# Transposing x in the DMA crossbar and splitting the w1 stream over two queues, in a squared-ReLU MLP kernel

## Chip, cores, metric

One core of one Trainium2 chip. The metric is device time in microseconds (us), median over runs. The profiler's span (first to last instruction) is about 2 us shorter than the time.

## The reference

```python
# x [1,2048,576]  w1 [576,4608]  b1 [4608]  w2 [4608,576]  b2 [576], all bf16
h = einsum("bsd,df->bsf", x, w1) + b1
h = relu(h) ** 2
out = einsum("bsf,fd->bsd", h, w2) + b2
```

x is cut into 4 blocks of 512 rows. For block n, phase An makes `hT` (the squared activations, features on partitions) and phase Bn multiplies by w2.

## The kernel before

576 is 9 chunks of 64, so phase A works with pairs of 64-row matmuls. `w1_h` holds the left 2304 columns of w1 on partitions 0 to 63 and the right 2304 on partitions 64 to 127. A step j makes 128 columns of each half:

```python
for c in range(NC):                       # NC = 9
    nc.tensor.matmul(bx[:], lhsT=w1_h[0:H, c, j*P:(j+1)*P], rhs=xT[0:H, c + 1, :], ...)
    nc.tensor.matmul(by[:], lhsT=w1_h[H:P, c, j*P:(j+1)*P], rhs=xT[H:P, c, :], ...)
```

Every 64-row chunk of x must thus lie transposed on both partition halves. The kernel before makes that with TensorE transposes of overlapping 128-column windows: 10 per row tile for blocks 0 and 1, and, for blocks 2 and 3, 5 per row tile plus two duplicating DMAs for every two row tiles, put into the middle of B0 and B1. All w1 loads go through one queue, in column order, lower half then upper half:

```python
def load_w1(j0, j1):
    for h in range(2):
        nc.sync.dma_start(out=w1_h[h*H:(h+1)*H, :, j0*P:j1*P],
                          in_=w1_v[:, :, h*FH + j0*P:h*FH + j1*P])
for (j0, j1) in [(0, 1), (1, 2), (2, 3), (3, 4), (4, 5), (5, 6)]:
    load_w1(j0, j1)
load_x_block(1, (nc.sync, nc.sync))
for (j0, j1) in [(6, 9), (9, 12), (12, 15), (15, 18)]:
    load_w1(j0, j1)
...
for j in range(NJ0):           a_step(0, j)     # NJ0 = 6
...                                             # 40 transposes of block 1
for j in range(NJ0, NJ1):      a_step(0, j)     # then A0 and A1 share each w1 column
for j in range(NJ0, NJ1):      a_step(1, j)
for j in range(NJ1, NJ):       a_step(0, j); a_step(1, j)
...
```

## Time and profile before

| | before |
|---|---|
| time, median (range) | 299.62 us (299.22 to 299.81) |
| span | 297.5 us |
| first phase-A matmul | 7.4 us |
| A0 with A1 | 73.2 us |
| B0, B1 | 36.5, 36.5 us |
| B2 with B3 | 70.7 us |

The page of the kernel before: busy time of each engine, TensorE's granted clock in tenths over 40 slices of the span, the DMA rate in the same slices, the queues, and the chain of work that ended last.

```profile
span 297.5 us, 5808 instructions
PE 292.7 (98%) x2574; PEld 184.8 (62%) x2574; DVE 79.0 (27%) x187; ACT 102.1 (34%) x161; POOL 8.9 (3%) x25
PEclk9999999999999999999999999999999999999999
GB/s 179 222 207 202 287 357 319 4 2 0 2 31 31 59 22 15 7 0 3 0 2 57 44 20 22 20 2 0 2 0 2 20 22 21 2 20 22 20 22 21
...
q1 hardware_dynamic: 21056, 15.19, 20.7%
q0 software_dynamic: 480, 1.19, 2.0%
...
PE 98%; DVE 0%; ACT 0%; issue 0%
```

TensorE (PE) is the bound: it has 98% of the chain, and no other engine reaches 1%. Only work taken from PE, without a new wait for it, can pay. The list of PE's waits says the same; its columns are total us, number of waits, longest:

```profile
PE wps L81 <- DVE wz L77: 1.3, 1, 1.3
PE ph L175 <- DVE xTw L128: 0.2, 1, 0.2
```

PE's transposes are what can be taken away. From the chain in order of time (start us, us, what), B0 with two of its transpose bursts:

```profile
80.57 4.52 PE po L198 x36
85.08 0.56 PE tp L148 x10
85.64 8.82 PE po L198 x72
94.46 0.56 PE tp L148 x10
95.02 22.05 PE po L198 x180
```

### The profile page before, as it was taken

The numbers are of one execution on the slowest core, as the hardware profiler recorded it, in microseconds if no ns is written. First come the engines' busy times: TensorE is split into PE (matmuls) and PEld (weight loads), VectorE is DVE, ScalarE is ACT, GpSimd is POOL, SyncE is SP. The second block draws the span as 40 slices with busy tenths as digits, with TensorE's granted clock in tenths as the row PEclk, the third lists the DMA queues.
The fourth block names the chain that finished last, engine by engine and source line by source line (L and its number), as shares of the span: only waits on it lengthen the run. The fifth ranks groups of instructions, "written<-read, shape, count | busy, mean of one in ns | idle before, by whom it ended". The sixth has DMA issues, their size and how long they took to land.

```text
span 297.5 us, 5808 instructions
## 1 busy us (share of the span) xinstructions
PE 292.7 (98%) x2574; PEld 184.8 (62%) x2574; DVE 79.0 (27%) x187; ACT 102.1 (34%) x161; POOL 8.9 (3%) x25
## 2 busy tenths in 40 slices
PE   7999999999999999999999999999999999999995
PEld 5564444444488876444468887544447778777774
DVE  3353444444401111444431001244441111101111
ACT  4575666666611000666641100266661000000000
POOL 3000000000010100000001100000000000000000
PEclk9999999999999999999999999999999999999999
DMA  8999999000011200000002200000000000000000
GB/s 179 222 207 202 287 357 319 4 2 0 2 31 31 59 22 15 7 0 3 0 2 57 44 20 22 20 2 0 2 0 2 20 22 21 2 20 22 20 22 21
DMA packets 21849, 17.04 MB, mean 57 GB/s; under 512 B 7924, under 2 KB 21504, under 8 KB 21824
## 3 DMA queue, kind: packets, MB, share of 16 engines
q1 hardware_dynamic: 21056, 15.19, 20.7%
q0 software_dynamic: 480, 1.19, 2.0%
q8 instruction: 20, 0.33, 0.5%
q10 hardware_dynamic: 288, 0.30, 0.3%
q14 instruction: 5, 0.04, 0.0%
HBM read 13.13 MB, written 2.36 MB: 52 GB/s over the span
## 4 chain that ended last, share of the span: by engine, by line
PE 98%; DVE 0%; ACT 0%; issue 0%
PE po L198 48%; PE ph L175 27%; PE ph L177 20%; PE tp L138 1%; PE wps L81 1%; PE tp L148 1%; ACT r L181 0%; ACT xTw L126 0%; DVE xTw L128 0%; DVE o_sb L207 0%; DVE wz L77 0%
## 5 line engine op out<-in xcount | busy, mean ns | idle before, releaser
L198 PE MATMUL po<-w_sb,hT 128*128 128x288 bf16 x1152 | 142.3, 286 | 0.0
L175 PE MATMUL ph<-xTw,w_h 64*128 64x512 bf16 x648 | 140.7, 376 | 0.2 <-DVE xTw L128 0.2
L177 PE MATMUL ph<-xTw,w_h 64*128 64x512 bf16 x648 | 140.5, 376 | 0.0
L198 PEld LDWEIGHTS <-hT 128*128 128x128 bf16 x1152 | 112.3, 98 | 29.3 <-issue 1.3
L181 ACT ACTIVATE r<-ph,b1T 128x512 bf16<-128x512 f32 x144 | 91.2, 684 | 95.0 <-PE ph L177 74.2
L175 PEld LDWEIGHTS <-w_h 64*128 64x128 bf16 x648 | 60.7, 94 | 43.9 <-issue 0.5
L182 DVE TENSOR_TENSOR hT<-r 128x512 bf16<-128x512 bf16 x144 | 61.2, 425 | 83.2 <-ACT r L181 83.1
L177 PEld LDWEIGHTS <-w_h 64*128 64x128 bf16 x648 | 60.6, 94 | 32.1 <-issue 0.2
L207 DVE TENSOR_TENSOR o_sb<-po,b_bc 128x288 bf16<-128x288 f32 x32 | 13.2, 452 | 127.3 <-PE po L198 127.3
L126 ACT COPY xTw<-tp 128x640 bf16<-128x640 bf16 x15 | 9.6, 695 | 26.0 <-PE tp L148 23.5
L154 POOL DMA_DIRECT2D xTw<-xTw x4 | 2.5, 627 | 141.2 <-ACT xTw L126 141.2
L138 PEld LDWEIGHTS <-x_sb 128*128 128x128 bf16 x80 | 5.7, 112 | 1.6 <-POOL warm L108 0.9
L138 PE MATMUL tp<-ident,x_sb 128*128 128x128 bf16 x80 | 6.1, 244 | 0.1
L128 DVE COPY xTw<-tp 128x640 bf16<-128x640 bf16 x9 | 4.3, 490 | 4.5 <-PE tp L138 4.2
L81 PE MATMUL wps<-wz 128*128 128x512 bf16 x5 | 2.3, 629 | 1.3 <-DVE wz L77 1.3
L148 PE MATMUL tp<-ident,x_sb 128*128 128x128 bf16 x40 | 2.9, 219 | 0.0
L155 POOL DMA_DIRECT2D xTw<-xTw x4 | 2.7, 676 | 0.0
L148 PEld LDWEIGHTS <-x_sb 128*128 128x128 bf16 x40 | 2.6, 98 | 0.2
L81 PEld LDWEIGHTS <-wz 128*128 128x128 bf16 x5 | 0.6, 134 | 2.1 <-DVE wz L77 1.3
L109 ACT ACT_TABLE_LOAD x1 | 1.3, 1283 | 1.7 <-PEq L284 1.7
L63 POOL MEMSET x_sb<- 128x256 bf16 x4 | 1.3, 319 | 18.8 <-PE tp L138 14.6
L64 POOL MEMSET x_sb<- 128x256 bf16 x4 | 1.3, 318 | 0.0
(14 smaller groups left out, 2.9 us busy)
## 6 DMA issues: line engine op xcount, KB each, us to landing
w_sb<-in_w_dram SPq DMA_DIRECT2D x6, 864.0 KB, 11.4
w_h<-in_w_dram SPq DMA_DIRECT2D x8, 432.0 KB, 11.7
out_dram<-o_sb SPq DMA_DIRECT2D x15, 144.0 KB, 1.8
w_h<-in_w_dram SPq DMA_DIRECT2D x12, 144.0 KB, 4.2
x_sb<-in_x_dram SPq DMA_DIRECT2D x6, 288.0 KB, 8.0
xTw<-xTw POOLq DMA_DIRECT2D x4, 160.0 KB, 2.6
xTw<-xTw POOLq DMA_DIRECT2D x4, 128.0 KB, 2.4
x_sb<-in_x_dram SPq DMA_DIRECT2D x2, 144.0 KB, 2.9
```

The costliest lines, as they stand in the source:

```text
L81: nc.tensor.matmul(wps[:], lhsT=wz[:, 0:P], rhs=wz[:, P:640], start=(i == 0), stop=(i == NWARM - 1))
L126: last_act_copy[0] = nc.scalar.copy(out=dst, in_=src)
L128: nc.vector.tensor_copy(out=dst, in_=src)
L138: nc.tensor.transpose(tp[:, i, :], xs[:, j, w * H:w * H + P], ident[:])
L148: nc.tensor.transpose(tp[:, n, :], xs[:, j, w * H:w * H + P], ident[:])
L155: eng.dma_start(out=xv[H:P, 0:NH, 0, cols], in_=xv[0:H, 0:NH, 1, cols])
L175: nc.tensor.matmul(bx[:], lhsT=w1_h[0:H, c, j * P:(j + 1) * P], rhs=xT[0:H, c + 1, :], start=(c == 0), stop=(c == NC - 1))
L177: nc.tensor.matmul(by[:], lhsT=w1_h[H:P, c, j * P:(j + 1) * P], rhs=xT[H:P, c, :], start=(c == 0), stop=(c == NC - 1))
L181: nc.scalar.activation(out=r[:], in_=bank[:], func=ACT.Relu, bias=b1T[:, ft:ft + 1], scale=1.0)
L182: nc.vector.tensor_tensor(out=hT[:, ft, :], in0=r[:], in1=r[:], op=ALU.mult)
L198: nc.tensor.matmul(po[h][:, 0:DH], lhsT=hT[:, ft, jj * P:(jj + 1) * P], rhs=w2_sb[:, ft, h * DH:(h + 1) * DH], start=(i == 0), stop=(i == ...
L207: nc.vector.tensor_tensor(out=o_sb[:, h * DH:(h + 1) * DH], in0=po[h][:, 0:DH], in1=b2_bc[:, h * DH:(h + 1) * DH], op=ALU.add,)
```

## The change

Intent: take 88 of the 120 x transposes off TensorE. Blocks 1 to 3 are transposed by the DMA crossbar on their way from DRAM, and small copies fill the ninth window. Block 0 keeps TensorE, with 8 transposes a row tile. Phases run A0 A1 B0 A2 B1 A3 B2 B3, A0 and A1 no longer mixed. The w1 halves go to two queues, so as to load faster: lower on SP (`nc.sync`), upper on POOL (`nc.gpsimd`) after two chunks on ACT. In the diff, comments and the text in brackets stand for code that is left out.

```diff
-    for (j0, j1) in [(0, 1), (1, 2), (2, 3), (3, 4), (4, 5), (5, 6)]:
-        load_w1(j0, j1)
-    load_x_block(1, (nc.sync, nc.sync))
-    for (j0, j1) in [(6, 9), (9, 12), (12, 15), (15, 18)]:
-        load_w1(j0, j1)
+    CH = [(0, 1), (1, 2), (2, 4), (4, 6), (6, 10), (10, 14), (14, 18)]
+    for (j0, j1) in CH[:2]:
+        load_w1(nc.sync, 0, j0, j1)
+        load_w1(nc.scalar, 1, j0, j1)
+    for (j0, j1) in CH[2:]:
+        load_w1(nc.sync, 0, j0, j1)
+        load_w1(nc.gpsimd, 1, j0, j1)
 ...
+    def load_xT(sb):
+        alloc_xT(sb)
+        xT = xT_blk[sb]
+        rows = x2[sb * SB:(sb + 1) * SB, :]
+        nc.sync.dma_start_transpose(out=xT[:, 0:NK, :], in_=rows[:, 0:2 * H * NK])
+        nc.sync.dma_start_transpose(out=xT[:, NK:2 * NK, :], in_=rows[:, H:H + 2 * H * NK])
+        nc.sync.dma_start(out=xT[0:H, 2 * NK, :], in_=xT[H:P, 2 * NK - 1, :])
+        nc.sync.dma_start(out=xT[H:P, 2 * NK, :], in_=xT[0:H, 0, :])
 ...
+    # block 0, per row tile: 4 + 4 transposes, and copies of (128 x 512) and (64 x 128)
 ...
-    (A0 and A1 interleaved; make_mid: transposes of blocks 2, 3 inside B0, B1)
+    load_xT(1); (b2, w2 loads on SP); load_xT(2)
+    phase_a(0); phase_a(1)
+    phase_b(0, hTs[0]); load_xT(3)
+    phase_a(2); phase_b(1, hTs[1]); phase_a(3); phase_b(2, hTs[2])
     phase_b(3, hTs[3], last=True)
```

## The prediction

> **What bounds the kernel now.** TensorE. The page shows PE 98% busy (292.7 of 297.5 us) and the chain of waits 98% on PE, clock 1.0 throughout. Stages, from the chain in order of time: head to the first phase-A matmul 7.4 us; A0 with A1 73.1; B0 36.5; A2 35.1; B1 36.5; A3 35.1; B2+B3 70.7; tail 3. A matmul pair of phase A starts every 0.216 us, so 18 steps of 9 pairs are 34.95 us: A2 and A3 run at that pace. B2+B3 gives 35.35 us for a B phase without transposes.
>
> **What the change removes.** On PE: the 40 transposes of block 1 (A0+A1 take 73.1 us against 2 x 35.05: 3.0 us), the 40 of blocks 2 and 3 inside B0 and B1 (36.5 against 35.35 twice: 2.3 us; the chain shows four bursts of 0.56 us), and 8 of 40 in the head. All but the last sit on the critical path, because PE never idles there: **5.3 us**. Off the path go 10 ACT copies of 693 ns, 4 DVE copies, 8 memsets and POOL's 8 duplicating DMAs. Matmuls, B-phase additions and output stores stay.
>
> **What it adds.** *Head:* the ninth window is now made by separate small copies. DVE copies of 128x640 took 490 ns; I estimate 0.42 us for 128x512 and 0.2 for 64x128, five of each: 3.1 us against 2.5. ACT likewise three pairs, estimated 0.85 us each against 0.69. DVE becomes the pacer from 4.35 us on and uses up what 8 fewer transposes give; ACT's windows are read only from the fifth pair on. Head: 0 to +0.2 us.
>
> *w1:* A0 now runs alone, so it consumes 288 KB a step of 1.94 us, 148 GB/s, until 42 us, where before A1 steps halved the need. The table of windows shows 216 GB/s from 7.4 to 19.1 us. Each load wrote 64 partitions. The Trainium skill, "SBUF — State Buffer" (Door 1: The DMA port swizzle), says that 64 partitions reach 8 of 16 ports, about 218 GB/s; the 216 agrees. The halves on two queues can use both sets. The tightest chunk is columns 6 to 10: 3.5 MB with x block 0; at 216 GB/s landed near 20 us, needed near 19; at 280 GB/s landed near 16. I expect no stall or under 1 us.
>
> *Crossbar:* 1.05 MB per block. "DMA: Bandwidth & Descriptors" (Latency and other measured facts) gives 261 GB/s, hence an estimate of 4 us a block, plus two dependent copies of about 2.5 us (POOL's landed in that). Block 1 is wanted at 42 us, block 2 at 114, block 3 at 186: tens of us of slack. SP waits for the transposes before issuing w2, which is needed from 77 us and took 14 us of issue. Off the path.
>
> **Sum.** 299.76 - 5.3 + 0.1 (head) + 0.0 to 0.8 (stall, mean 0.1): **294.6 us**, 1.7% faster; range **293.4 to 296.8**. Chances: faster by over 2% 0.12, within 2% 0.83, slower 0.05.
>
> **What would show each step.** Right: PE transposes fall from 120 (plus b1) to 32; A0+A1 last about 70.1 us, B0 and B1 35.35 each, A2 and A3 unchanged; the first phase-A matmul starts at 7.3 to 7.7 us; crossbar transposes land long before their readers; DMA well over 216 GB/s in 7 to 20 us; PE never idle in the body. Wrong: PE waits on w1 inside A0, or on transposed x at 42 us.
>
> **What would make it wrong.** (a) POOL-issued w1 loads lagging behind SP's, stalling A0 near chunks 2-4 or 6-10: +1 to +4 us. (b) Crossbar transposes many times slower than estimated, or slowing the w1 stream. (c) A stall long enough to lower the granted clock. (d) PE starting earlier than I think, by up to 0.6 us, which without a stall comes close to the 2% line (293.8).

## The result, and the profile after

| | before | after |
|---|---|---|
| time, median (range) | 299.62 us (299.22 to 299.81) | 305.22 us (303.38 to 305.25) |
| span, mean granted clock | 297.5 us, 1.000 | 303.4 us, 0.989 |
| first phase-A matmul | 7.4 us | 8.6 us |
| A0 with A1 | 73.2 us | 79.6 us |
| B0, B1 | 36.5, 36.5 us | 35.4, 35.4 us |

The ratio is 1.017, interval 1.014 to 1.020. The kernel got slower: the change is clear of noise and of the other sign than predicted, but under 2%; the time lies outside the predicted range.

The same parts of the page, after:

```profile
span 303.4 us, 5600 instructions
PE 289.3 (95%) x2486; PEld 178.2 (59%) x2486; DVE 78.3 (26%) x188; ACT 95.1 (31%) x152; POOL 5.3 (2%) x14
PEclk9968999999999999999999999999999999999999
GB/s 185 229 213 172 175 338 352 146 158 9 2 0 2 19 22 19 22 0 3 2 0 2 19 22 19 19 2 2 0 2 0 22 19 23 0 22 19 22 19 19
...
q1 hardware_dynamic: 24688, 14.31, 20.2%
q0 software_dynamic: 704, 2.37, 3.4%
q10 hardware_dynamic: 1472, 0.59, 0.9%
...
PE 92%; DMA 6%; DVE 0%; issue 0%
PE po L176 47%; PE ph L156 45%; DMA w_h<-in_w_dram 5%; DMA x_sb<-in_x_dram 1%; PE ph L158 1%; DVE o_sb L185 0%
```

The clock falls in slices 3 and 4, and w1 loads have come onto the chain. The waits of PE, after:

```profile
PE ph L156 <- DMA w_h<-in_w_dram: 9.2, 3, 5.7
PE wps L73 <- DVE wz L69: 1.3, 1, 1.3
```

All of it lies in A0's first columns. PE's timeline, where only lines that begin after idle time are copied (last bracket: us idle before, and who ended it):

```profile
8.59 0.39 PE L156 MATMUL ph<-xTw,w_h 64*128 64x512 bf16 x1 [2.74 <-DMA w_h<-in_w_dram]
...
11.38 0.39 PE L156 MATMUL ph<-xTw,w_h 64*128 64x512 bf16 x1 [0.68 <-DMA w_h<-in_w_dram]
...
19.24 0.61 PE L156 MATMUL ph<-xTw,w_h 64*128 64x512 bf16 x1 [5.74 <-DMA w_h<-in_w_dram]
```

The wait at 19.24 us is the one for chunk 2-4. After it a matmul takes 0.61 us: the clock is at half. B0 and everything after A0 run as predicted; in the chain, B0 is now one unbroken piece:

```profile
88.16 35.39 PE po L176 x288
123.54 0.32 PE ph L156
```

When did each w1 chunk land? These times come from the semaphore that each load raises (issue, then landing, in us; needed is when PE would read it at full pace from 7.3 us on):

```
columns   lower half (SP)     upper half             needed
0-1        1.66 ->  8.54      ACT   1.67 ->  7.72      7.3
1-2        2.44 -> 11.33      ACT   2.38 -> 10.06      9.2
2-4        3.61 -> 19.19      POOL  2.20 ->  7.99     11.2
4-6        4.25 -> 21.89      POOL  2.95 -> 11.05     15.1
6-10       4.95 -> 24.95      POOL  3.68 -> 14.82     18.9
10-14      7.62 -> 28.85      POOL  4.40 -> 17.74     26.7
14-18     14.77 -> 30.77      POOL  5.13 -> 20.67     34.5
```

POOL's upper halves come early, and SP's lower halves come late. I had named "POOL-issued w1 loads lagging behind SP's" as a risk. It is the reverse. Counting the trace's DMA packets by queue shows why; between 12 and 18 us:

```
SP    333 packets, mean  492 B,  27 GB/s
POOL  329 packets, mean 3686 B, 202 GB/s
```

The two queues get the same number of packets and very unequal bytes. The Trainium skill, "DMA: Bandwidth & Descriptors" (Queues, rings and completion order), says that a DMA engine goes round its queues packet by packet. The near-equal counts agree. The page's queue lines show the sizes: q0 (POOL's queue) moved 2.37 MB in 704 packets, about 3.4 KB each; q10 (ACT's) 0.59 MB in 1472, about 0.4 KB. A packet of SP or ACT holds one contiguous run, and one of POOL gathers several, up to 4 KB here.

**Theory T1**: turns are taken by packet, so POOL's big packets starve SP's small ones; PE waits for SP's half, and the long wait halves the clock. **Rivals**: R1, A0 without A1 needs w1 faster than any one queue brings it (the order is at fault); R2, the crossbar transposes on SP slow the w1 stream; T1b, any second queue starves SP, whatever its packets; T1c, SP starves because the other queue is filled early with later columns.

### The profile page after: what moved, and what is told of

Its sections match the earlier page's. It is cut to its first block, busy times and chain, and to the rows that moved or that the text cites. A ratio compares the mean times of both kernels' runs of the same rounds, so it can differ in the third digit from the quotient of the medians.

```text
span 303.4 us, 5600 instructions
## 1 busy us (share of the span) xinstructions
PE 289.3 (95%) x2486; PEld 178.2 (59%) x2486; DVE 78.3 (26%) x188; ACT 95.1 (31%) x152; POOL 5.3 (2%) x14
## 3 DMA queue, kind: packets, MB, share of 16 engines
q0 software_dynamic: 704, 2.37, 3.4%
q10 hardware_dynamic: 1472, 0.59, 0.9%
## 4 chain that ended last, share of the span: by engine, by line
PE 92%; DMA 6%; DVE 0%; issue 0%
PE po L176 47%; PE ph L156 45%; DMA w_h<-in_w_dram 5%; DMA x_sb<-in_x_dram 1%; PE ph L158 1%; DVE o_sb L185 0%
## 5 line engine op out<-in xcount | busy, mean ns | idle before, releaser
L156 PE MATMUL ph<-xTw,w_h 64*128 64x512 bf16 x648 | 143.4, 381 | 9.2 <-DMA w_h<-in_w_dram 9.2
L158 PE MATMUL ph<-xTw,w_h 64*128 64x512 bf16 x648 | 143.4, 382 | 0.0
L156 PEld LDWEIGHTS <-w_h 64*128 64x128 bf16 x648 | 61.2, 95 | 88.7 <-DMA w_h<-in_w_dram 10.3
L158 PEld LDWEIGHTS <-w_h 64*128 64x128 bf16 x648 | 61.4, 95 | 0.0
L65 POOL DMA_DIRECT2D w_h<-in_w_dram x5 | 3.7, 780 | 0.0
L123 DVE COPY xTw<-ta 128x512 bf16<-128x512 bf16 x4 | 1.7, 425 | 3.0 <-PE ta L122 2.9
L132 ACT COPY xTw<-tb 128x512 bf16<-128x512 bf16 x3 | 1.8, 585 | 0.4 <-PE tb L127 0.4
L122 PE MATMUL ta<-ident,x_sb 128*128 128x128 bf16 x16 | 1.8, 242 | 0.0
L127 PE MATMUL tb<-ident,x_sb 128*128 128x128 bf16 x16 | 1.7, 239 | 0.0
L122 PEld LDWEIGHTS <-x_sb 128*128 128x128 bf16 x16 | 1.2, 109 | 0.8 <-DMA x_sb<-in_x_dram 0.8
L127 PEld LDWEIGHTS <-x_sb 128*128 128x128 bf16 x16 | 1.3, 111 | 0.0
L124 DVE COPY xTw<-ta 64x128 bf16<-64x128 bf16 x4 | 0.9, 218 | 0.1
L133 ACT COPY xTw<-tb 64x128 bf16<-64x128 bf16 x3 | 0.8, 262 | 0.0
```

The costliest lines, as they stand in the source:

```text
L65: eng.dma_start(out=w1_h[h * H:(h + 1) * H, :, j0 * P:j1 * P], in_=w1_v[:, :, h * FH + j0 * P:h * FH + j1 * P])
L122: nc.tensor.transpose(ta[:, k, :], xs[:, j, 2 * H * k:2 * H * k + P], ident[:])
L123: nc.vector.tensor_copy(out=xT0[:, 0:NK, cols], in_=ta[:, :, :])
L127: nc.tensor.transpose(tb[:, k, :], xs[:, j, H + 2 * H * k:H + 2 * H * k + P], ident[:])
L132: nc.scalar.copy(out=xT0[:, NK:2 * NK, cols], in_=tb[:, :, :])
L156: nc.tensor.matmul(bx[:], lhsT=w1_h[0:H, cl, j * P:(j + 1) * P], rhs=xT[0:H, wl, :], start=(i == 0), stop=(i == NC - 1))
```

## The experiments

All eight gave outputs that agree with the reference. Kernels of one set shared a chip and the runs of the kernel before.

### e1_all_sp: all w1 on SP

```diff
-        load_w1(nc.scalar, 1, j0, j1)
+        load_w1(nc.sync, 1, j0, j1)
 ...
-        load_w1(nc.gpsimd, 1, j0, j1)
+        load_w1(nc.sync, 1, j0, j1)
```

> The changed kernel with all w1 halves on SP, in column order, same chunks. Theory T1 (the POOL queue's packets of about 3.7 KB take turns one for one with SP's packets of about 0.5 KB, so SP's lower halves starve): the waits at columns 2-4 vanish; first phase-A matmul at 7.3 to 7.7 us; at 195 to 200 GB/s chunk 6-10 lands near 20 us against a need at 19, so at most about 1.5 us of stall; no half clock; 294.3 to 296.0 us. Rival R1 (A0 alone needs w1 faster than any single queue brings it, so the A0-first order is at fault): stalls of 4 us or more remain, 299 us or more. Rival R2 (the crossbar transposes on SP slow w1): unchanged stalls, since the transposes stay on SP.

Measured: 295.52 us (294.59 to 296.30), before 299.91; ratio 0.986 (0.983 to 0.988). Clock 1.0. The first phase-A matmul starts at 7.23 us and the waits at columns 0 to 2 are gone. PE's waits:

```profile
PE ph L158 <- DMA w_h<-in_w_dram: 1.6, 1, 1.6
PE wps L73 <- DVE wz L69: 1.3, 1, 1.3
PE ph L156 <- DVE xTw L123: 0.6, 1, 0.6
```

The wait of 1.6 us is for chunk 6-10, whose upper half landed at 20.83 us. Order and crossbar are as in the change, so R1 and R2 fall as the main cause: at most this 1.6 us can be R1's.

### e2_swap: lower half on ACT and POOL, upper on SP

```diff
 (two lines joined into one)
-        load_w1(nc.sync, 0, j0, j1);  load_w1(nc.gpsimd, 1, j0, j1)
+        load_w1(nc.sync, 1, j0, j1);  load_w1(nc.gpsimd, 0, j0, j1)
 (the first two chunks likewise, with nc.scalar)
```

> The changed kernel with the halves swapped: lower on ACT and POOL, upper on SP. T1: the same stall, now for the upper half; 303 to 306.5 us, POOL's chunks land by about 21 us in order while SP's chunk 2-4 lands near 19 us. A rival that blames the lower half's partitions or its place in DRAM expects a clearly different time (under 300).

Measured: 306.19 us (304.89 to 307.35), ratio 1.023. SP's chunk 2-4, now the upper half, landed at 19.23 us; POOL's landed in order by 21.20. PE now waits mostly at L158, the upper matmul (5.9 us), where in the change it waited at L156. From 12 to 18 us SP had 333 packets and POOL 330. The queue decides, not the half.

### e3_before_pool: the kernel before, upper halves on POOL

```diff
-            nc.sync.dma_start(out=w1_h[h * H:(h + 1) * H, ...
+            eng = nc.gpsimd if h == 1 and j0 >= 2 else nc.sync
+            eng.dma_start(out=w1_h[h * H:(h + 1) * H, ...
```

> The kernel before with one thing changed: upper w1 halves from column 2 on go to POOL's queue. T1: SP's lower halves starve in it too: PE waits for w1 at column 2, half clock after it if the wait is over about 3 us, 303 to 311 us. R1 (order at fault) and R2 (crossbar at fault): nothing of either is in this kernel, so 299 to 301 us.

Measured: 310.65 us (308.52 to 311.04), ratio 1.035. This one edit costs the kernel before 10.7 us: PE waits 7.8 us for w1 where it waited for none, and the clock halves in the longest wait, of 3.98 us:

```profile
PE ph L176 <- DMA w_h<-in_w_dram: 5.8, 2, 4.0
PE ph L178 <- DMA w_h<-in_w_dram: 2.0, 2, 1.8
```

From 14 to 19 us SP sends runs of 256 B, and it had 268 packets and 13.6 GB/s against POOL's 249 and 200. The stall needs neither the new order nor the crossbar.

### e4_act: chunks 2-4 and 4-6 of the upper half on ACT, the later ones on SP

```diff
-        load_w1(nc.gpsimd, 1, j0, j1)
+        load_w1(nc.scalar if j0 < 6 else nc.sync, 1, j0, j1)
```

> The changed kernel with upper chunks 2-4 and 4-6 on ACT's queue (packets of the same size as SP's) and the later ones on SP. T1: both halves of 2-4 land within 1.5 us of each other at about 10 to 12 us, no half clock, 294.3 to 297 us. A rival T1b (any second queue starves SP, whatever the packet size): SP's 2-4 lands after 15 us, over 300 us. For the step of the prediction that two queues reach more ports: over 230 GB/s between 5 and 12 us if true, about 200 if not.

Measured: 295.53 us (294.95 to 295.67), ratio 0.986. Chunk 2-4 landed at 10.23 (SP) and 11.06 us (ACT), 4-6 at 12.73 and 14.00. T1b falls: a second queue with packets of SP's size takes its share and no more. PE never waited for w1; it waited 0.9 us once for an ACT copy, which ACT's longer issuing had delayed. The total was 230 GB/s from 4 to 6 us, 195 from 6 to 8 and 215 from 8 to 12, hardly above one queue's 203, so the gain in rate that I had expected from two queues did not show here.

### e5_fine: all w1 on SP, in finer chunks

```diff
 (on e1_all_sp)
-    CH = [(0, 1), (1, 2), (2, 4), (4, 6), (6, 10), (10, 14), (14, 18)]
+    CH = [(0, 1), (1, 2), (2, 3), (3, 4), (4, 5), (5, 6),
+          (6, 8), (8, 10), (10, 12), (12, 14), (14, 16), (16, 18)]
```

> All w1 on SP as in e1_all_sp, with one column a load up to column 6 and two after that. T1: e1's only stall (1.6 us before column 6) came from the four-column chunk that must land whole; at 200 GB/s columns 6-8 now land near 17 us against a need at 18.9, so PE never waits for w1; 293.4 to 294.7 us, which is what the prediction's sum gave without its stall term (294.5). If A0-first order were at fault beyond chunk size, a stall of 1 us or more stays, over 295.

Measured: **293.78 us** (293.72 to 293.92), before 299.93; ratio 0.980 (0.978 to 0.982). It is faster than the kernel before, clear of noise; whether by 2% is unclear, since the interval holds 0.98. Lines of the page, the list of PE's waits, and lines of the chain: the start of A0, then those that begin where A1, B0 and A2 end:

```profile
span 292.0 us, 5608 instructions
PEclk9999999999999999999999999999999999999999
PE 97%; DVE 1%; issue 0%
```

```profile
PE wps L73 <- DVE wz L69: 1.3, 1, 1.3
PE ph L156 <- DVE xTw L123: 0.6, 1, 0.6
```

```profile
7.28 0.37 PE ph L156
...
77.39 35.39 PE po L176 x288
112.78 0.32 PE ph L156
...
147.85 35.39 PE po L176 x288
```

No wait for w1 is left (chunk 6-8 landed by 18.03 us, needed at 18.9), so R1 falls altogether: A0 alone is served by one queue at about 200 GB/s, if the chunks are small enough to land in time.

### e6_keep_clock: dummy matmuls in the stall

```diff
 (on the change, in phase_a)
+            if sb == 0 and j == 2:
+                fill = ps_o.tile([P, 512], FP32, name="fill", tag="po")
+                for i in range(26):
+                    nc.tensor.matmul(fill[:], lhsT=wz[:, 0:P], rhs=wz[:, P:640], ...)
             a_step(sb, j)
```

> The changed kernel with 26 dummy matmuls (26 x 0.216 = 5.6 us of work on zeros) put between columns 1 and 2 of A0, in the time that TensorE idled. If the half clock after the stall is caused by the idle time and costs what I worked out (12.5 pairs of 0.427 against 0.216 us, 2.65 us): clock 1.0 throughout, 302.0 to 303.4 us. If the idle time is not its cause: 305 or more.

Measured: 302.88 us (302.57 to 304.06), ratio 1.011; mean clock 0.998. In another set the change itself took 305.22 (its ratio 1.017). B0 started at 86.11 us against 88.16, although SP's chunk 2-4 landed 0.66 us later in this run (19.85 against 19.19). So the idle time causes the half clock, and keeping PE busy returns 2 to 3 us of the loss. It does not return the wait. The Trainium skill, "TensorE: Matmul & The Clock Gate" (Part 1), says that an idle window of about 3.4 us puts the clock to half. The runs agree in the main: idle times of 5.74 us (the change) and 3.98 us (e3) were followed by half clock, those of 2.74 and 1.8 us were not. The figure is not a sharp limit: the clock fell 4.4 us into the idle time of the change, and 2.7 us into that of e3 (at 22.26 us, PE idle since 19.54). In the change the clock is 0.99 in the first of these stretches, in whose last 4.5 us PE idles, and 0.50 in the second:

```profile
12.00:18.00 6.00, 1.50 (x14) 0.49 (x10) 1.28 (x3) 1.26 (x2) 0.00 (x0) 0.99 1.06 229
18.00:20.00 2.00, 0.76 (x4) 0.28 (x6) 0.00 (x0) 0.00 (x0) 0.00 (x0) 0.50 1.12 217
```

(Columns of this table of windows: stretch, its length, busy us with instruction counts of PE, PEld, DVE, ACT and POOL, granted clock, DMA share, GB/s.)

### m1_meter: the queues by themselves

```diff
 (on e1_all_sp, added at the end; the results of these loads are not read; some lines joined)
+    halves(nc.sync, [], nc.sync, QS);  all_parts()      # QS: four chunks of 1 KB runs
+    halves(nc.sync, QS, nc.scalar, QS);  all_parts()    # halves: 64 partitions each
+    halves(nc.sync, QS, nc.gpsimd, QS);  all_parts()    # all_parts: 1 KB runs, 128 partitions
+    halves(nc.sync, [(2, 18)], nc.gpsimd, QS)           # SP: 4 KB runs
```

> Not a candidate: e1_all_sp, and after the last output w1 is loaded again in groups, to meter the queues (the time is over 60 us longer; outputs stay right). (1) upper half alone on SP, 1 KB runs: 190 to 200 GB/s. (2) the same runs over 128 partitions, SP alone: about 350 GB/s if the number of partitions limits group 1, about 200 if the 1 KB runs of DRAM do. (3) lower on SP beside upper on ACT: 300 GB/s or more if the halves on two queues use both port sets as the prediction had it; about 200 to 220 if not. (4) lower on SP in 1 KB runs beside upper on POOL: if turns are taken by packet, equal packet counts, POOL 3.5 to 4 KB a packet and SP 1 KB, so SP gets about a fifth. (5) lower on SP in 4 KB runs beside POOL: SP's share rises to 45 to 55% by the same rule; if POOL has priority for another reason, SP stays near a fifth.

The groups did not run one after the other: each load waited only for its own columns, and the first began at 199 us, so its time (323.40 us) means nothing and its groups overlapped. I read stretches, picked after the run, in which the packet records show the named queues alone. GB/s by queue:

```
SP alone, 64 partitions, 1 KB runs (222-223 us)        193
SP alone, 128 partitions, 1 KB runs (220-221 us)       381
SP beside ACT, 1 KB runs each (235-237 us)             184 + 186
SP 1 KB beside POOL (276-278): 99 and 92 packets        50 + 188
SP 4 KB beside POOL (310-312): 83 and 85 packets       170 + 174
```

In the fourth row 34 of SP's 99 packets are output stores, of 1152 B; the rest are loads. Single microseconds scatter: SP alone with 64 partitions also shows 253 GB/s (202-203 us). Over longer stretches the rates are steady: 202 from 14 to 20 us of e1_all_sp (64 partitions), 357 from 46 to 50 us of e5_fine (w2, 128 partitions).

The totals of four of these stretches in the table of windows:

```profile
220.00:221.00 1.00, 1.00 (x13) 0.47 (x10) 0.00 (x0) 0.00 (x0) 0.00 (x0) 1.00 1.08 381
235.00:237.00 2.00, 2.00 (x13) 0.79 (x10) 0.43 (x1) 0.08 (x1) 0.40 (x1) 0.50 1.07 370
276.00:278.00 2.00, 2.00 (x19) 1.58 (x17) 0.00 (x0) 0.00 (x0) 0.00 (x0) 1.00 1.03 239
310.00:312.00 2.00, 2.00 (x19) 1.58 (x17) 0.00 (x0) 0.00 (x0) 0.00 (x0) 1.00 1.02 344
```

The last two lines are the direct test of T1. With 1 KB packets SP got 21% of the bytes beside POOL; with 4 KB packets it got 49%. The packet counts were near equal both times. POOL has no priority; it has larger packets. The first line shows, against 193 GB/s, that 64 partitions had half the rate of 128; the second, that two queues of equal packets can have both halves' rates at once.

### e8_act_all: every upper half on ACT

```diff
-        load_w1(nc.gpsimd, 1, j0, j1)
+        load_w1(nc.scalar, 1, j0, j1)
 ...
-        if j == 0:      # which engine makes block 0's second copies
+        if True:        # always DVE: ACT is busy issuing
```

> The changed kernel with every upper w1 half on ACT's queue in place of POOL's, all queued early as POOL's were, and the head's ACT copies moved to DVE (ACT is busy issuing until about 12 us). Packets of both queues are then of one size. T1: SP's lower halves keep step with ACT's upper ones, within 1.5 us at each chunk, 2-4 near 10 to 12 us and 6-10 by 20 us. A rival T1c (SP starves because the other queue is filled early with later columns, whatever its packets): SP's 2-4 lands after 15 us. Port step: once both queues send 1 KB runs (from about 13 us), the total is 300 GB/s or more if the halves fall out of step over the ports, about 210 if they run in lockstep. Time 294 to 298 us, the head's DVE copies and late activations costing 1 to 3 us.

Measured: 297.00 us (296.81 to 297.73), ratio 0.991. SP and ACT landed chunk 2-4 at 10.03 and 11.68 us, 6-10 at 18.53 and 17.64; the largest gap was 2.1 us (10-14), a little over the 1.5 expected. ACT's issuing was slow, so that its chunks from 6 on were queued at 6.58 to 11.70 us, not at 3.68 to 5.13 like POOL's. But from 16 to 22 us all of them were queued, and SP still got half: T1c falls. One thing is not as T1 would have it: from 12 to 14 us SP had 27 packets of data and ACT 414, although SP's chunks 6-10 and 10-14 had been issued at 7.31 and 8.65. The even turns between SP and ACT begin at about 14 us; what held SP back before that stays open. The loss against e5_fine is the head, where phase A starts at 8.59 us behind the longer row of DVE copies instead of 7.28, and 1.8 us of waiting for a late activation. The port step of the prediction comes out split:

```profile
8.00:12.00 4.00, 3.41 (x32) 1.84 (x33) 1.57 (x6) 0.00 (x0) 0.00 (x0) 1.00 1.23 226
16.00:22.00 6.00, 6.00 (x59) 4.50 (x56) 2.57 (x7) 3.82 (x7) 0.00 (x0) 1.00 1.09 349
```

With 512 B runs in both queues the total is 226 GB/s; with 1 KB runs in both it is 349, of which SP has 177 and ACT 170. Why the 512 B runs do not add up in the same way stays open; between 8 and 12 us the two queues led by turns (SP's packets against ACT's, in half microseconds: 50 to 167 from 8.5 us, 163 to 48 from 9.5).

## Why the prediction was wrong

**Right: what the change removes.** In e5_fine, where nothing waits for w1, A0+A1 take 77.39 - 7.28 = 70.11 us (predicted "about 70.1"), B0 and B1 35.39 (predicted 35.35). Against the kernel before that is 3.05 + 2 x 1.11 = 5.3 us, the predicted saving. The head starts phase A at 7.28 us (predicted 7.3 to 7.7). The sum without its stall term was 299.76 - 5.3 + 0.1 = 294.5; e5_fine took 293.78.

**Right by luck: the crossbar off the path.** The prediction gave it "tens of us of slack". Block 1's transposes landed at 33.0 and 35.2 us in the change and its last copy at 42.3; A1 starts at about 53 us there (88.16 less 35.05 for one A phase), but only because A0 had stalled. In e5_fine the last copy was issued at 37.26 us, as the w2 loads began, and landed at 43.83: 6.6 us, not "about 2.5". A1 starts at 42.25 there, and the ninth pair of its first step, the first to read that copy, at 43.97. The slack was 0.14 us. An A0 quicker by more than that, all else the same, would have made PE wait for it.

**Wrong: the step "I expect no stall or under 1 us"**, and the term "0.0 to 0.8 (stall, mean 0.1)" in the sum. It measured 10.8 us, the difference in B0's start between the change and e5_fine (88.16 - 77.39). It is made of:

- first phase-A matmul late: 8.59 - 7.28 = 1.3 us;
- the wait at column 1: the matmul starts are 1.05 us apart instead of 0.21, 0.8 us;
- the wait at column 2: 6.12 us apart instead of 0.22, 5.9 us;
- the half clock: 38 matmuls start from 19.24 to 26.0 us, 6.76 us; at full pace 38 x 0.108 = 4.1; 2.7 us.

These add up to 10.7 us. The stall follows from SP's lower halves landing late, and e1, e2, e3, e4, e8 and the meter show that this follows from packet size in the turns between the queues.

**What I missed.** I reasoned about the total rate ("at 216 GB/s landed near 20 us") and let it serve the chunks in column order. The total was indeed 229 GB/s from 12 to 18 us. But two queues are not one order: POOL's columns 14-18 landed at 20.7 us, 14 us ahead of their need, while SP's columns 2-4 landed at 19.2 us, 8 us behind theirs. The column order that the kernel before had from its single queue was worth more than a second queue.

**The port step.** "The halves on two queues can use both sets" holds where packets are equal and of 1 KB (349 GB/s, e8). In the change it could not pay: packet turns fixed the bytes at about 7.4 to 1 (202 to 27 GB/s). POOL's 202 is near the 193 to 203 that one queue had on 64 partitions elsewhere, so I take it for its limit; POOL alone on 64 partitions was not measured. My mark for this step, "DMA well over 216 GB/s in 7 to 20 us", was not met: 225. And the 216 itself was not w1 alone: part of that stretch is the load of x block 1, over 128 partitions (268 GB/s from 13 to 16 us); from 7.4 to 11.5 us, with w1 alone, it was 195.

**Mis-sized.** The half clock was named as risk (c), and "+1 to +4 us" for a w1 stall was too small by more than half. The crossbar moved 221 GB/s over 26 to 30 us of e8, not the 261 taken from the skill's page; this did no harm.

## What to carry to other kernels

A stream that feeds a consumer in order should stay in one queue, or in queues whose packets are of one size: in these runs a load on POOL's queue beside small-run loads on SP took most of the bandwidth and delivered its own later pieces first. Check each chunk's landing against the time that it is needed, not the mean rate against the mean need, for small dependent copies too (e5_fine escaped a wait by 0.14 us), and make the chunks before a tight deadline small. A wait of 4 to 6 us on TensorE cost more than itself, since the half clock afterwards added 2.7 us here.

## What the Trainium skill lacked or had wrong

- "DMA: Bandwidth & Descriptors" (Rules for kernel authors) says of two transfers to disjoint partition halves that they serialize, so "Don't bother". With 1 KB runs, halves on SP and ACT ran together at 349 GB/s (e8) and 370 GB/s (meter), against 193 to 203 for one queue. With 512 B runs it nearly held: 226.
- The same page (Queues, rings and completion order) has the turns by packet, which the counts of POOL and SP bear out (333 to 329). What it lacks is that the packets of SP and ACT held one run each here, while POOL's gathered 4096 B (4608 B in e3), and what follows from it: POOL left SP 27 of 229 GB/s where SP sent runs of 512 B, 14 of 214 with 256 B, 50 of 239 with about 1 KB, and half with 4 KB.
- The same page (Rules for kernel authors) says that spreading DMAs over SP, ACT and GpSimd doesn't help bandwidth. Here it could help (349 GB/s) and it could reorder the stream and cost 10.7 us.
- "SBUF — State Buffer" (Door 1: The DMA port swizzle) was right on 64 partitions: 193 GB/s, against 381 for the same run length over 128 (stretches of 1 us), or 202 against 357 over longer ones.
- 261 GB/s for a DMA transpose ("DMA: Bandwidth & Descriptors", Latency and other measured facts): transposes, from DRAM in packets of about 256 B, ran at 221 GB/s (e8, 26 to 30 us).
